# Opening of a fused LSH-attention and soft-MoE kernel: one load moves to ScalarE's queue, a cut at column 256, two spreads behind the shift's row, first maxima in the banks of two pools

## The chip, the cores and the metric

The kernel runs on one core of a Trainium2 chip. The metric is the device time of one execution in microseconds (us). A profiled execution has a span, from its first to its last instruction, and a time of its own, which is a little longer than the span. Engines are named as in the profile: PE (TensorE matmul), PEld (its weight loads), DVE (VectorE), ACT (ScalarE), POOL (GpSimd), SP (SyncE, which only issues DMAs here).

## The reference

There are 4 batches of 8 heads, 768 positions and 64 columns per head. For each head, positions are hashed to 6 bits, a query sees only keys of its own bucket, and the softmax output of the heads feeds a soft mixture of 8 experts with 4 slots each.

```python
q_bits = (np.einsum('bhsd,dk->bhsk', q, proj) > 0).astype(np.int64)
k_bits = (np.einsum('bhsd,dk->bhsk', k, proj) > 0).astype(np.int64)
...
mask = q_bucket[:, :, :, None] == k_bucket[:, :, None, :]
scores = scale * np.matmul(q, k.transpose(0, 1, 3, 2))
scores = np.where(mask, scores, -1000000000.0)
scores = scores - np.max(scores, axis=-1, keepdims=True)
attn = np.exp(scores)
attn = attn / (np.sum(attn, axis=-1, keepdims=True) + 1e-09)
return np.matmul(attn, v).astype(np.float32)
...
logits = x @ phi
...
slot_input = d.T @ x
...
h = np.maximum(slot_input[e] @ w1[e], 0.0)
slot_out[e] = h @ w2[e]
...
return (c @ slot_out).astype(np.float32)
```

## The kernel before

The 32 heads (4 batches times 8) are numbered h = 0 to 31 and are worked on one after the other, a pair (h, h+1) per load of q and k. Of each head, q and k are split into a high and a low part. They stand in two tiles, Y and X, which share one buffer `XY` per head; three such buffers (XY0, XY1, XY2) rotate, so heads 0 and 3 share XY0. Rows 64 to 79 of Y hold the hash bits in a form that pushes pairs of different buckets far down in the score.

For one head the steps are these. `smax` (line 463) makes a first, approximate score product on PE, 512 or 256 columns at a time, and DVE takes the largest value of each row (lines 477 and 480). `shift` (line 484) turns the maxima into one number per query on DVE (lines 489 to 492). `shift_rows` (line 496) transposes these numbers on PE (line 499), copies them with ACT into `mr` (line 502) and sends them by a DMA (`move`, line 379) into row 64 of the head's X and Y. This transfer is called the shift's row below, "XY<-mr" in the trace. Only then can `scores` (line 515 on PE, the exponential on ACT in line 519) start, since the row is part of its operands. `acc` (POOL) adds the row sums, `av` (line 544) multiplies with v.

Operands come to a head's buffer by DMAs that SP issues: `load` brings q and k of a pair (line 255), `spread_y`, `spread_l` and `spread_x` move parts of the stage into XY, `spread_bits` moves the bits from `bt` in four transfers, `load_v` brings v. SP takes them in the order in which they are issued in the program. An issue occupies SP's queue for some time, and an issue that waits holds all that stand behind it.

The order of the work is set by two tables, `STEADY` and `ONCE`, which give each call of a step a place in time; `at` looks a call up and the plan is sorted by that number. Entries far below zero belong to the opening, which is the time until head 0 has its maxima. Every engine gets its instructions in the order of the sorted plan.

In the opening the first pair is loaded in four halves (`load_half`, line 257): rows 0 to 63 (head 0) of k and of q, then rows 64 to 127 (head 1). `first_copy` (ACT, line 429) copies head 0's halves into Y. `first_bits` (line 435) projects them to bits on PE, 512 columns and then 256, and `first_over` (DVE, line 406) compares the result with the threshold and writes rows 64 to 79 of Y. `more_bits` (line 411) does the bits of both heads in one go. `first_hi` (ACT, line 440) and `split_lo` (POOL, line 375) make the high and low parts, and `first_x` (ACT, line 403) copies two of them into X. Between the steps, `spin` runs matmuls on a tile of ones that nobody reads, seven at the start and one or more after each maximum of head 0, so that PE has work.

The names in the trace: `st`, `smx`, `mi`, `av` are accumulation tiles in PSUM from the pools p_st (3 banks), p_sm (2), p_mi (2) and p_av (1); `mx` holds maxima, `stage` the raw and split q and k.

Of the kernel before, what the change touches and what calls it, by code (L numbers as in the profile page):

```python
# [9 lines left out]
F32 = mybir.dt.float32  # L10
F32R = mybir.dt.float32r
# [5 lines left out]
B, H, S, D, NB = 4, 8, 768, 64, 6  # L17
BH = B * H
P = 128
# [72 lines left out]
    ('first_copy', 1): -118.0, ('first_hi', 0): -107.0, ('first_hi', 1): -108.0, ('first_mz',): -96.0,  # L92
    ('first_over', 0, 0, 256): -110.0, ('first_over', 0, 256, 512): -100.0, ('first_over', 0, 512, 768): -99.0,
    ('first_over', 1, 0, 512): -111.0, ('first_over', 1, 512, 768): -109.0, ('first_rows', 0): -115.0,
    ('first_rows', 1): -114.0, ('first_rows', 2): -25.530842, ('first_x', 0): -83.0, ('first_x', 1): -78.0,
    ('keep_warm', 'c'): 195.7225, ('load', 10): 39.299177, ('load', 12): 51.299177, ('load', 14): 63.299177,
# [52 lines left out]
    ('spread_bits', 31): 174.191023, ('spread_bits', 4): 13.138864, ('spread_bits', 9): 42.191023,  # L149
    ('spread_l', 0): -91.0, ('spread_l', 1): -82.0, ('spread_l', 2): 1.51245, ('spread_l', 3): 6.331558,  # L150
    ('spread_x', 0): -87.0, ('spread_x', 1): -10.012043, ('spread_x', 2): 8.862333, ('spread_x', 3): 6.703225,
    ('spread_y', 1): -105.0, ('spread_y', 2): -86.0, ('spread_y', 25): 138.143568, ('spread_y', 27): 150.143568,
    ('spread_y', 29): 162.143568, ('spread_y', 3): 3.806412, ('spread_y', 31): 174.143568,
# [36 lines left out]
def lsh_attention_soft_moe(  # L190
# [11 lines left out]
    nc = tc.nc  # L202
# [43 lines left out]
    raw = stage[:, 0:2]  # L246
# [10 lines left out]
    def load_half(a):  # L257
        for x in (1, 0):
            nc.sync.dma_start(out=raw[D * a:D * a + D, x], in_=qk[x, 0, D * a:D * a + D])

# [4 lines left out]


    ones = cp.tile([P, 32], F32, name="ones")
    nc.vector.memset(ones, 1.0)
    XYs = [held.tile([P, 2, 2, S], F32R, name=f"XY{i}") for i, held in enumerate((yp, xp, yq))]
    Xs, Ys = [[t[:, :, n] for t in XYs] for n in range(2)]  # L270
    idle = Xs[2][:, 0, 0:P + 512]
    nc.vector.memset(idle.bitcast(F32), 1.0)
    eps = cp.tile([P, 1], F32, name="eps")
# [45 lines left out]

    def spin(n, cols=512):  # L320
        pt = p_av.tile([P, 512], F32, name="av")
        for _ in range(n):
            nc.tensor.matmul(pt[:, 0:cols], idle[:, 0:P], idle[:, P:P + cols], start=True, stop=True)

    spin(7)


# [93 lines left out]

    first_pt = {}

    def first_over(x, a, b):
        j = 2 * x + a // 512
        over(Ys[0][64:80, x, a:b], first_pt[x], slice(32 * j, 32 * j + 16), cols=slice(a % 512, a % 512 + b - a))

# [3 lines left out]
    def first_bits(x):  # L431
        first_pt[x] = p_st.tile([P, 512], F32, name="st")
        for c, (a, b) in enumerate(((0, 512), (512, S))):
            j = 2 * x + c
            nc.tensor.matmul(first_pt[x][32 * j:32 * j + 32, 0:b - a], pb[0:D, 32 * x:32 * x + 32], raw[0:D, x, a:b],
                             start=True, stop=True)
# [26 lines left out]
    def smax(h, t, part):  # L463
# [6 lines left out]
        if key not in s:  # L470
            s[key] = p_sm.tile([P, 512], F32, name="smx")
        pt = s[key]
# [8 lines left out]
        if h == 0 and t < NT - 1:  # L481
            spin(1)

# [381 lines left out]
    for n in (1, 0):  # L865
        at(first_copy, n)
        at(first_bits, n)
        at(first_hi, n)
    for xab in ((1, 0, 512), (0, 0, 256), (1, 512, S), (0, 256, 512), (0, 512, S)):
        at(first_over, *xab)  # L870
    at(more_bits)
    for n in range(3):
        at(spin, 2, tag=n)
    at(bits_rest)
# [264 lines left out]
```

## Time and profile before

| What | us |
|---|---|
| timed runs | 472.23, 474.15, 2233.8 |
| median of the three | 474.15 |
| profiled execution, its own time | 471.47 |
| its span | 469.7 |

Busy shares of the span are 97% for PE, 83% for DVE, 70% for POOL and 53% for ACT. The largest of the timed runs is far from all others, and the median of three is therefore one of two ordinary runs; the profiled execution is the lowest of the ordinary ones. The trace gives, for each instruction, its start from the beginning of the span, its duration, how long its engine was idle before it, and what ended that idle time.

### The profile page before, as it was taken

The page shows a single profiled execution, that of the slowest core. Times are in us where ns is not written, and L with a number is a line of the kernel's source. Part 1 is how long each engine was busy: PE and PEld are TensorE (multiplying, and loading weights), DVE is VectorE, ACT ScalarE, POOL GpSimd, SP SyncE. Part 2 cuts the span into 40 slices and gives each one's busy share as a digit, 9 for nine tenths or more (in the row PEclk, how much of TensorE's full clock was granted, in tenths as well). Part 3 has the DMA queues.
Part 4 walks back from the last instruction along what each step waited for, and adds up shares of the span by engine and source line. Part 5 has one row for each costly group of instructions (what it writes and reads, how often), then busy time and mean ns, then how long its engine had stood idle before and what let it go on. Part 6 is the DMA issues. An engine that isn't in the chain of part 4 may idle for free.

```text
span 469.7 us, 10655 instructions
## 1 busy us (share of the span) xinstructions
PE 456.4 (97%) x3980; PEld 287.8 (61%) x3980; DVE 389.0 (83%) x723; ACT 247.4 (53%) x462; POOL 327.6 (70%) x205
## 2 busy tenths in 40 slices
PE   7999999999999999999999999999999999999993
PEld 3565666666666666666656666666666666553472
DVE  7868898989798988889898989897979886787952
ACT  5364556464657555555556464646565545531242
POOL 7878778878775988787868987787759878810000
PEclk9999999999999999999999999999999999999998
DMA  5757677777774767878683878685846677899997
GB/s 159 200 139 165 162 170 230 163 238 164 218 172 150 170 194 165 238 167 241 145 235 106 205 203 202 206 202 159 200 135 166 177 180 258 297 387 409 408 365 305
DMA packets 39535, 99.29 MB, mean 211 GB/s; under 512 B 7326, under 2 KB 13612, under 8 KB 39484
## 3 DMA queue, kind: packets, MB, share of 16 engines
q1 hardware_dynamic: 39292, 98.16, 72.3%
q8 instruction: 31, 0.51, 0.4%
q10 hardware_dynamic: 160, 0.39, 0.4%
q14 instruction: 20, 0.16, 0.1%
q0 software_dynamic: 32, 0.07, 0.0%
HBM read 52.76 MB, written 6.29 MB: 126 GB/s over the span
## 4 chain that ended last, share of the span: by engine, by line
PE 91%; DVE 3%; DMA 2%; issue 1%; ACT 0%; SPq 0%; DVEq 0%; ACTq 0%
PE st L515 29%; PE av L544 25%; PE smx L474 16%; PE qs L1050 3%; PE qh L1000 3%; PE mi L556 2%; PE mi L411 2%; PE mi L607 2%; PE mi L572 2%; DMA XY<-mr 1%; PE mi L592 1%; DMA stage<-qk 1%; PE mi L762 1%; PE mi L499 1%; PE qh L1070 1%
## 5 line engine op out<-in xcount | busy, mean ns | idle before, releaser
L532 POOL TENSOR_TENSOR acc<-acc,pt 128x768 f32<-128x768 f32 x125 | 229.1, 1833 | 9.6
L519 ACT ACTIVATE pt<-st 128x512 f32<-128x512 f32 x288 | 164.3, 597 | 62.3 <-PE st L515 56.5
L515 PE MATMUL st<-XY 128*128 128x256 f32 (+1 forms) x768 | 178.0, 347 | 0.7 <-DMA XY<-mr 0.7
L480 DVE TENSOR_REDUCE mx<-smx 128x1 f32<-128x512 f32 x192 | 131.1, 688 | 24.9 <-PE smx L474 22.8
L515 PEld LDWEIGHTS st<-XY 128*128 128x128 f32 x768 | 125.0, 189 | 19.0 <-ACT pt L519 1.7
L544 PE MATMUL av<-pt,v 128*32 128x384 f32 x1536 | 133.1, 486 | 0.0
L474 PE MATMUL smx<-XY 96*128 96x512 f32 (+1 forms) x384 | 118.4, 357 | 1.2 <-DVE mx L477 0.9
L526 POOL TENSOR_TENSOR acc<-pt 128x768 f32<-128x768 f32 x32 | 58.9, 1839 | 53.1 <-ACT pt L519 53.1
L544 PEld LDWEIGHTS av<-pt,v 128*32 128x32 f32 x1536 | 49.7, 110 | 72.8 <-issue 71.6
L474 PEld LDWEIGHTS smx<-XY 96*128 96x128 f32 x384 | 66.0, 188 | 30.8 <-issue 9.6
L477 DVE TENSOR_REDUCE mx<-smx 128x2 f32<-128x512 f32 x96 | 65.8, 686 | 6.1 <-PE smx L474 5.5
L548 ACT COPY avs<-av 128x384 f32<-128x384 f32 x32 | 15.3, 477 | 82.9 <-PE av L544 82.8
L564 DVE RECIPROCAL dl<-sm 128x128 f32<-128x128 f32 x45 | 38.8, 915 | 13.9 <-ACT sm L559 10.1
L372 DVE TENSOR_REDUCE stage<-stage 128x768 fp32r<-128x1536 f32 x28 | 49.0, 1782 | 0.0
L365 ACT ACTIVATE stage<-stage 128x768 fp32r<-128x768 f32 x28 | 22.6, 836 | 5.3 <-DMA stage<-qk 3.8
L609 DVE TENSOR_TENSOR xq<-mi,r 128x256 f32<-128x256 f32 x45 | 17.4, 416 | 1.1 <-PE mi L607 1.1
L833 DVE STREAM_TRANSPOSE w<-call 32x256 f32<-32x256 f32 (+2 forms) x48 | 14.9, 333 | 1.7 <-PE qh L1000 1.1
L1050 PE MATMUL qs<-w 128*32 128x128 f32 (+1 forms) x352 | 15.3, 303 | 0.0
L607 PE MATMUL mi<-ident,avs 128*128 128x128 f32 x90 | 14.8, 272 | 0.0
L607 PEld LDWEIGHTS mi<-ident,avs 128*128 128x128 f32 x90 | 11.7, 140 | 4.0
L1050 PEld LDWEIGHTS qs<-w 128*32 128x32 f32 x352 | 10.6, 110 | 5.2 <-issue 2.2
L411 PE MATMUL mi<-stage,pb 128*32 128x384 f32 x120 | 12.8, 498 | 0.7 <-DMA stage<-qk 0.7
(183 smaller groups left out, 330.8 us busy)
## 6 DMA issues: line engine op xcount, KB each, us to landing
w<-w SPq DMA_DIRECT2D x53, 512.0 KB
XY<-stage SPq DMA_DIRECT2D x62, 384.0 KB
XY<-stage SPq DMA_DIRECT2D x62, 192.0 KB
stage<-qk SPq DMA_DIRECT2D x28, 384.0 KB
v<-vt SPq DMA_DIRECT2D x32, 192.0 KB
out<-stage SPq DMA_DIRECT2D x12, 512.0 KB
stage<-w SPq DMA_DIRECT2D x7, 512.0 KB
xq<-w SPq DMA_DIRECT2D x3, 512.0 KB
```

Source lines behind the costliest of these rows:

```text
L372: nc.vector.tensor_reduce(out=w[:, 2 * x + 1], in_=stage[:, x:n + 1:n - x].rearrange("p t s -> p s t"), axis=AX.X, op=ALU.add, negate=True)
L474: nc.tensor.matmul(pt[:, o:o + b - a], Ys[h % N_Y][0:96, 0, t * P:(t + 1) * P], Ys[h % N_Y][0:96, 1, a:b], start=True, stop=True)
L477: nc.vector.tensor_reduce(out=mx[:, n - 1:n + 1], in_=pt.rearrange("p (a x) -> p a x", a=2), axis=AX.X, op=ALU.max)
L480: nc.vector.reduce_max(out=mx[:, n:n + 1], in_=pt, axis=AX.X)
L515: nc.tensor.matmul(pt[:, o:o + b - a], x[:, 1, i * P:(i + 1) * P], x[:, 0, a:b], start=first, stop=not first)
L519: nc.scalar.activation(pts[i // 2][:, 512 * u:512 * u + 512], pt, AF.Exp, scale=D ** -0.5)
L526: nc.gpsimd.tensor_tensor(out=s["acc"], in0=pr[:, 0:S], in1=pr[:, S:2 * S], op=ALU.add)
L532: eng.tensor_tensor(out=s["acc"], in0=s["acc"], in1=pr[:, a * S:(a + 1) * S], op=ALU.add)
L544: nc.tensor.matmul(s["av"][D * c + d:D * c + d + 32, 0:HC], s["v"][:, i, d:d + 32], pr[:, o + c * HC:o + (c + 1) * HC], start=(i == 0), st ...
L564: nc.vector.reciprocal(out=st[h]["rs"][:, k * P:(k + 1) * P], in_=st[h]["sm"][:, k * P:(k + 1) * P])
L607: nc.tensor.transpose(pt[:, o:o + P], st[h + a]["avs"][:, k * P:(k + 1) * P], ident)
L1050: nc.tensor.matmul(po[32 * j:32 * j + 32], hTs[g][:, f, 32 * j:32 * j + 32], wt[1, x, 2 * g + f // 4, j].rearrange("p (f m) -> p f m", f=4 ...
```

## The change

Five things are edited, all in the first 20 us of the program:

1. The first half of k is loaded from ACT's DMA queue; the three other halves stay on SP's queue.
2. The bits of q are cut at column 256 and not at 512: PE projects 256 columns and then 512, and DVE's second comparison is one of 512 columns and not two of 256.
3. In the table, `spread_l` of head 1 and `spread_y` of head 2 come behind the shift's row of head 0 on SP's queue and not ahead of it, and the first of the two `first_x` copies comes ahead of ACT's two spreads.
4. The maxima of head 0 take their banks from p_sm and p_st in turn and not from p_sm alone.
5. The spins are 256 columns wide and twice as many; the tile of ones for them is filled first and is smaller.

```diff
-    ('spread_l', 0): -91.0, ('spread_l', 1): -82.0, ('spread_l', 2): 1.51245, ('spread_l', 3): 6.331558,
+    ('spread_l', 0): -91.0, ('spread_l', 1): -45.0, ('spread_l', 2): 1.51245, ('spread_l', 3): 6.331558,
...
     def load_half(a):
         for x in (1, 0):
-            nc.sync.dma_start(out=raw[D * a:D * a + D, x], in_=qk[x, 0, D * a:D * a + D])
+            eng = nc.scalar if x > a else nc.sync
+            eng.dma_start(out=raw[D * a:D * a + D, x], in_=qk[x, 0, D * a:D * a + D])
...
-    idle = Xs[2][:, 0, 0:P + 512]
+    idle = Xs[2][:, 0, 0:P + 256]
...
-    def spin(n, cols=512):
+    def spin(n, cols=256):
...
-    spin(7)
+    spin(14)
...
+    first_cuts = (0, 256, S), (0, 512, S)
 
     def first_over(x, a, b):
-        j = 2 * x + a // 512
-        over(Ys[0][64:80, x, a:b], first_pt[x], slice(32 * j, 32 * j + 16), cols=slice(a % 512, a % 512 + b - a))
+        c = first_cuts[x][1] <= a
+        j, o = 2 * x + c, a - first_cuts[x][c]
+        over(Ys[0][64:80, x, a:b], first_pt[x], slice(32 * j, 32 * j + 16), cols=slice(o, o + b - a))
...
-        for c, (a, b) in enumerate(((0, 512), (512, S))):
+        for c, (a, b) in enumerate(zip(first_cuts[x], first_cuts[x][1:])):
...
         if key not in s:
-            s[key] = p_sm.tile([P, 512], F32, name="smx")
+            pool = p_st if h == 0 and (key[1] + key[2]) % 2 else p_sm
+            s[key] = pool.tile([P, 512], F32, name=names[pool])
...
         if h == 0 and t < NT - 1:
-            spin(1)
+            spin(2)
...
-    for xab in ((1, 0, 512), (0, 0, 256), (1, 512, S), (0, 256, 512), (0, 512, S)):
+    for xab in ((1, 0, 512), (0, 0, 256), (1, 512, S), (0, 256, S)):
```

On SP's queue, around the shift's row of head 0. In the kernel before, XY_98, XY_99 and XY_100 are XY0, XY1 and XY2; the rows follow the load of `cst`:

```order
L379 DMA XY_99<-bt 13x384 x2
L379 DMA XY_99<-bt 12x384 x2
L379 DMA XY_100<-stage 64x2x768
L379 DMA XY_99<-stage 32x2x768
L379 DMA XY_98<-mr 1x12x128
L255 DMA stage<-qk 128x768 x2
```

In the changed kernel, where XY_96, XY_97 and XY_98 are XY0, XY1 and XY2:

```order
L380 DMA XY_97<-bt 13x384 x2
L380 DMA XY_97<-bt 12x384 x2
L380 DMA XY_96<-mr 1x12x128
L380 DMA XY_97<-stage 32x2x768
L380 DMA XY_98<-stage 64x2x768
L255 DMA stage<-qk 128x768 x2
```

The row of head 0 has moved ahead of the two spreads, which now stand between it and the load of the next pair; all that follows on SP is in the same order as before.

On DVE, from the first comparison of the bits to the fifth reduction of head 0. Before:

```order
L406 TENSOR_SCALAR XY_98<-st,con 16x512
L406 TENSOR_SCALAR XY_98<-st,con 16x256 x2
L480 TENSOR_REDUCE mx<-smx 128x1
L406 TENSOR_SCALAR XY_98<-st,con 16x256 x2
L477 TENSOR_REDUCE mx<-smx 128x2
L480 TENSOR_REDUCE mx<-smx 128x1 x2
L477 TENSOR_REDUCE mx<-smx 128x2
```

In the changed kernel:

```order
L407 TENSOR_SCALAR XY_96<-st,con 16x512
L407 TENSOR_SCALAR XY_96<-st,con 16x256 x2
L484 TENSOR_REDUCE mx<-smx 128x1
L407 TENSOR_SCALAR XY_96<-st,con 16x512
L481 TENSOR_REDUCE mx<-st 128x2
L484 TENSOR_REDUCE mx<-smx 128x1
L484 TENSOR_REDUCE mx<-st 128x1
L481 TENSOR_REDUCE mx<-smx 128x2
```

Two comparisons of 256 columns have become one of 512, and every second tile of maxima is an st tile.

## Rows read from the trace of the kernel before

**Rows 1.** Window: length; busy time by engine (instructions); granted clock; DMA share; GB/s.

```profile
44.00:419.00 375.00, 374.89 (x3136) 241.76 (x3137) 322.79 (x573) 210.98 (x395) 292.31 (x179) 1.00 0.71 194
```

**Rows 2.** Chain that ended last, 17 to 45: start, duration, what.

```profile
37.55 0.24 ACT mr L502
...
38.06 5.75 DMA XY<-mr
```

**Rows 3.** Timeline of PE: start, duration, operation, idle time before it.

```profile
43.85 0.73 PE L515 MATMUL st<-XY 128*128 128x512 f32 x2 [0.70 <-DMA XY<-mr]
```

**Rows 4.** Timeline of SP's queue, 0 to 46: start, duration of the issues.

```profile
1.18 2.49 SPq L259 DMA_DIRECT2D stage<-qk  x4
...
15.54 1.50 SPq L379 DMA_DIRECT2D XY<-stage  x2
18.04 0.82 SPq L379 DMA_DIRECT2D XY<-mr  x1
18.96 0.92 SPq L255 DMA_DIRECT2D stage<-qk  x2
19.97 3.26 SPq L379 DMA_DIRECT2D XY<-bt  x4
23.28 0.51 SPq L351 DMA_DIRECT2D v<-vt  x1
23.84 3.30 SPq L379 DMA_DIRECT2D XY<-stage  x3
27.24 0.83 SPq L379 DMA_DIRECT2D XY<-mr  x1
28.17 0.68 SPq L379 DMA_DIRECT2D XY<-stage  x1
28.89 4.36 SPq L379 DMA_DIRECT2D XY<-bt  x4
33.29 4.67 SPq L379 DMA_DIRECT2D XY<-stage  x5
38.06 1.80 SPq L379 DMA_DIRECT2D XY<-mr  x1
```

**Rows 5.** Waits of SP's queue, 0 to 45: total, times, longest.

```profile
SPq L379 <- ACT mr L502: 0.9, 1, 0.9
```

**Rows 6.** Chain that ended last, 0 to 44: its first steps.

```profile
3.08 4.29 DMA stage<-qk
7.41 0.85 PE mi L411 x8
```

**Rows 7.** Timeline of DVE, 6 to 21.

```profile
9.46 1.09 DVE L406 TENSOR_SCALAR XY<-st,con 16x256 fp32r<-16x256 f32 x2
...
12.76 0.69 DVE L477 TENSOR_REDUCE mx<-smx 128x2 f32<-128x512 f32 x1 [0.21 <-PE smx L474]
...
14.99 0.69 DVE L477 TENSOR_REDUCE mx<-smx 128x2 f32<-128x512 f32 x1 [0.25 <-PE smx L474]
15.90 0.69 DVE L480 TENSOR_REDUCE mx<-smx 128x1 f32<-128x512 f32 x1 [0.22 <-PE smx L474]
```

**Rows 8.** Groups of DVE by form, 6 to 18: busy us, mean ns, idle before.

```profile
L406 DVE TENSOR_SCALAR XY<-st,con 16x512 fp32r<-16x512 f32 x1 | 0.8, 807 | 1.3 <-ACT XY L429 1.3
```

**Rows 9.** Windows of two microseconds, columns as in rows 1.

```profile
4.00:6.00 2.00, 2.00 (x10) 0.63 (x9) 1.24 (x2) 1.43 (x2) 1.94 (x2) 1.00 1.01 230
...
23.00:25.00 2.00, 2.00 (x10) 1.50 (x9) 1.85 (x5) 1.79 (x4) 0.00 (x0) 1.00 0.26 68
...
35.00:37.00 2.00, 2.00 (x14) 1.77 (x13) 1.83 (x6) 1.89 (x4) 0.92 (x2) 1.00 0.94 203
```

**Rows 10.** Timeline of ACT, 0 to 22.

```profile
0.74 1.28 ACT L298 ACT_TABLE_LOAD   x1 [0.74 <-PEq L1130]
...
4.53 1.70 ACT L429 CAST XY<-stage 64x768 fp32r<-64x768 f32 x2 [1.74 <-DMA stage<-qk]
...
17.76 0.26 ACT L502 CAST mr<-mi 12x128 fp32r<-12x128 f32 x1 [1.43 <-PE mi L499]
```

More of the change, by code (lines that the diff above doesn't have):

```diff
@@ L92 @@
     ('first_copy', 1): -118.0, ('first_hi', 0): -107.0, ('first_hi', 1): -108.0, ('first_mz',): -96.0,
-    ('first_over', 0, 0, 256): -110.0, ('first_over', 0, 256, 512): -100.0, ('first_over', 0, 512, 768): -99.0,
+    ('first_over', 0, 0, 256): -110.0, ('first_over', 0, 256, 768): -100.0,
     ('first_over', 1, 0, 512): -111.0, ('first_over', 1, 512, 768): -109.0, ('first_rows', 0): -115.0,
-    ('first_rows', 1): -114.0, ('first_rows', 2): -25.530842, ('first_x', 0): -83.0, ('first_x', 1): -78.0,
+    ('first_rows', 1): -114.0, ('first_rows', 2): -25.530842, ('first_x', 0): -92.5, ('first_x', 1): -78.0,
     ('keep_warm', 'c'): 195.7225, ('load', 10): 39.299177, ('load', 12): 51.299177, ('load', 14): 63.299177,
@@ L149 @@
     ('spread_bits', 31): 174.191023, ('spread_bits', 4): 13.138864, ('spread_bits', 9): 42.191023,
-    ('spread_l', 0): -91.0, ('spread_l', 1): -82.0, ('spread_l', 2): 1.51245, ('spread_l', 3): 6.331558,
+    ('spread_l', 0): -91.0, ('spread_l', 1): -45.0, ('spread_l', 2): 1.51245, ('spread_l', 3): 6.331558,
     ('spread_x', 0): -87.0, ('spread_x', 1): -10.012043, ('spread_x', 2): 8.862333, ('spread_x', 3): 6.703225,
-    ('spread_y', 1): -105.0, ('spread_y', 2): -86.0, ('spread_y', 25): 138.143568, ('spread_y', 27): 150.143568,
+    ('spread_y', 1): -105.0, ('spread_y', 2): -44.9, ('spread_y', 25): 138.143568, ('spread_y', 27): 150.143568,
     ('spread_y', 29): 162.143568, ('spread_y', 3): 3.806412, ('spread_y', 31): 174.143568,
@@ L264, in lsh_attention_soft_moe @@
     vs = [held.tile([P, NT, D], F32, name=f"v{i}") for i, held in enumerate((ap, mp))]
+    XYs = [held.tile([P, 2, 2, S], F32R, name=f"XY{i}") for i, held in enumerate((yp, xp, yq))]
+    Xs, Ys = [[t[:, :, n] for t in XYs] for n in range(2)]
+    idle = Xs[2][:, 0, 0:P + 256]
+    nc.vector.memset(idle.bitcast(F32), 1.0)
     ones = cp.tile([P, 32], F32, name="ones")
     nc.vector.memset(ones, 1.0)
-    XYs = [held.tile([P, 2, 2, S], F32R, name=f"XY{i}") for i, held in enumerate((yp, xp, yq))]
-    Xs, Ys = [[t[:, :, n] for t in XYs] for n in range(2)]
-    idle = Xs[2][:, 0, 0:P + 512]
-    nc.vector.memset(idle.bitcast(F32), 1.0)
     eps = cp.tile([P, 1], F32, name="eps")
@@ L872, in lsh_attention_soft_moe @@
     for n in range(3):
-        at(spin, 2, tag=n)
+        at(spin, 4, tag=n)
     at(bits_rest)
```

## The prediction

> **What bounds the kernel now.** I began with the busy time by stretch. From 44 to 419 us PE is busy for 374.89 of 375.00 us [rows 1]: in four fifths of the span it waits for nothing, and the reader is to see that a gain of the opening reaches the end if, and only if, it reaches PE at 44 us. The change edits the first 20 us, so the question is what lies between.
>
> Next came the chain that ended last, between 17 and 45 us. It runs along PE, and then it has one large step that is not PE: 38.06 us, 5.75 us long, the shift's row of head 2 [rows 2]. On PE itself the same place shows as an idle time of 0.70 us in front of 43.85 us, ended by that transfer [rows 3]. So the scores of head 2 begin when a transfer lands, and PE would have been ready at 43.85 - 0.70 = 43.15 us.
>
> What sets that transfer? Its data were ready when ACT's copy ended, at 37.55 + 0.24 = 37.79 us [rows 2], and SP took it up at 38.06. The timeline of SP's queue tells why I don't read this as ACT's doing: from 18.96 to 38.06 us, which is 19.10 us, SP issues for 0.92 + 3.26 + 0.51 + 3.30 + 0.83 + 0.68 + 4.36 + 4.67 = 18.53 us [rows 4], and the issue before ended at 33.29 + 4.67 = 37.96 us. The queue is full from the load of the second pair on; what comes late at its beginning comes late at its end. In front of the row the DMA engines are full as well, with a share of 0.94 from 35 to 37 us [rows 9].
>
> The chain of the opening starts with the halves of q and k: the fourth lands at 3.08 + 4.29 = 7.37 us, and PE goes on with the bits at 7.41 us [rows 6].
>
> **The change part by part.** I count first what the row of head 0, issued at 18.04 us [rows 4], gains, and call that sum G.
>
> *The half of k on ACT's queue.* Four halves take 2.49 us of SP's queue, 0.62 us each [rows 4]; with one of them gone the last is issued 0.62 us earlier. That is the upper bound. The lower one comes from the DMA engines, which have a share of 1.01 from 4 to 6 us [rows 9]: if they are full from the first byte, all that helps is that the first byte is asked for at 0.74 us, where ACT's queue opens [rows 10], and not at 1.18 us [rows 4], 0.44 us. I take 0.55 us, between two ends that are close. On ACT the issue stands ahead of the table load, which would then start about 0.62 us later; ACT's copy of k waits 1.74 us for its data [rows 10], and that wait hides it.
>
> The Trainium skill, page "DMA: Bandwidth & Descriptors", section "Issuing engines are not separate DMA queues", says that DMAs started by different engines run on the same 16 DMA engines and that starting them from several engines saves only the time of starting them. By that rule alone this term would be 0.62 us, and the full share at 4 us speaks for less. With 0.62 the forecast below would fall by 0.07 us.
>
> *The cut at 256.* Two comparisons of 256 columns took 1.09 us [rows 7]; one of 512 columns takes 0.81 us [rows 8]. It stands between the first and the second maximum on DVE, which has work all along there: 0.28 us.
>
> *Two pools' banks.* What can go are DVE's waits for the next product, 0.21 + 0.25 + 0.22 = 0.68 us [rows 7]. The lower bound is 0, because the spins stand between the products as before and have as many columns (twice 256 for 512), so PE may set the same pace. I take the middle, 0.35 us: the bank was only one of two reasons.
>
> *The spins and ACT's copy.* The same columns, begun a little earlier: 0. The copy that goes ahead of ACT's spreads fills a stretch in which ACT waits; the row's copy on ACT waits 1.43 us for PE today [rows 10], so it costs nothing unless that wait is used up. 0.
>
> G = 0.55 + 0.28 + 0.35 = 1.18 us, with ends 0.44 + 0.28 + 0 = 0.72 and 0.62 + 0.28 + 0.68 = 1.58 us. The row of head 0 would be issued at 18.04 - 1.18 = 16.86 us.
>
> *The two spreads behind the row.* They took 1.50 us of SP's queue from 15.54 us on, and with the gap behind them 1.55 us [rows 4]. There they cost nothing, since SP then still waited 0.9 us for the row's data [rows 5]. Now SP waits idle and issues them after the row. Queued behind them is the load of the second pair, and behind that everything up to the row of head 2. The load, 0.92 us after the row today (18.96 - 18.04), now comes 0.92 + 1.55 us after it, at 16.86 + 2.47 = 19.33 us: 0.37 us **later** than before, though the row itself is 1.18 us earlier. The ends are 1.55 - 1.58 = -0.03 and 1.55 - 0.72 = +0.83 us.
>
> *From there to the end.* The full queue hands the 0.37 us on: the row of head 2 is issued at 38.43 and lands at 38.06 + 5.75 + 0.37 = 44.18 us. PE could start at 43.15 - 1.18 = 41.97 us at best and waits some 2.2 us instead of 0.70. All that head 0 won is given back there. Behind it PE is full as before, so the end moves by +0.37 us: 471.47 + 0.37 = 471.84 us for an execution like the profiled one (span 469.7, 1.8 us around it). The three ordinary runs shown are 471.47, 472.23 and 474.15 us; their middle one is 0.76 us above the profiled one, and the prediction is made for such a run: 472.23 + 0.37 = 472.6 us. By the ends of the sum alone it would lie between 472.2 and 473.1 us.
>
> **The rivals.**
>
> *The gain reaches the end.* If SP's queue has more slack than its issue times show (an issue of 1.80 us for a row of 12 pieces [rows 4] is time in which it was held up, not work), an earlier PE would bring the row of head 2 earlier, since its data were ready only 0.27 us before it was issued. Then the whole G stays: 472.23 - 1.18 = 471.05 us. For it speaks that the chain is PE and ACT up to 37.79 us [rows 2]; against it that the hold-ups come with a DMA share of 0.94 [rows 9], and the bytes in front of the row are as many as before and start later.
>
> *The transfers pile up, slower.* Place: the DMA engines behind the row of head 0. Until now they moved the two spreads while SP waited; now these start at about 16.86 + 0.92 = 17.8 us and not at 15.54, 2.24 us later, with the load right behind, and the bits of head 2 behind that. If nothing of this is made up, the row of head 2 lands 2.24 us later: 472.23 + 2.24 = 474.5 us. It decides once the pile is larger than the slack of the engines before 25 us; from 23 to 25 us their share is 0.26 [rows 9], which leaves 1.48 us. So most of it should be made up, and the price would be 0.76 us if the slack is used in full, hardly more than the forecast. For the full price the engines would have to be slow with small pieces there rather than idle.
>
> *The change doesn't do what it says.* The halves land no earlier, since two queues share the engines, and the spins keep PE's pace: G = 0.28 us, the load comes 1.55 - 0.28 = 1.27 us later, and the end is 472.23 + 1.27 = 473.5 us.
>
> **How the numbers follow.** I give the forecast 0.52, the gain that reaches the end 0.23, the pile 0.13, and no earlier landing 0.12. The likeliest case gives 472.6 us. The range must take in the first rival and the two slower ones with the scatter of single runs, 0.76 us below the middle one: 471.05 - 0.8 = 470.2 at the lower end, and 474.5 + 0.8 = 475.3 at the upper.
>
> About 2%, or 9.4 us, is what a measurement of this kernel can tell from no change. No case comes near it: all of the opening up to the row of head 0 is 18 us long and would have to be halved, or the stretch from 44 to 419 us, whose order of instructions the change leaves alone, would have to change. That gives 0.98 for within 2% and 0.01 for each side.
>
> **What would show it right or wrong.** In the profile of the changed kernel the row of head 0 should be issued between 16.5 and 17.3 us, the load of the second pair between 18.9 and 19.8 us, with SP idle for some 2 us ahead of the row. The row of head 2 should be issued at 38.0 us or later, and PE's idle time in front of its scores should have grown from 0.70 to about 2 us, now or spread over an earlier wait for the row of head 1. If the scores of head 2 start before 43.2 us, SP's queue was not the bound and the first rival holds. If PE waits at 25 us for the bits of head 2, or these scores start after 45 us, it is the pile. If the bits of both heads (the second line of rows 6) still start at 7.4 us, the halves did not land earlier. Any idle time of PE after 44 us that was not there before would make the step to the end wrong.

## The result: about 0.7% slower, and the profile after

| What | before | after |
|---|---|---|
| median of 12 runs, us | 471.82 | 475.95 |
| ratio, with its 95% interval | 1 | 1.0073 (1.0047 to 1.0098) |
| profiled execution, us | 471.47 | 474.60 |
| its span, us | 469.7 | 472.8 |

The forecast was 472.6 us, some 0.37 us above an ordinary run, with a range up to 475.3 us. The median of the changed kernel, 475.95 us, lies above that range; it is still within 2%. By the ratio the change costs 471.82 * 0.0073 = 3.4 us. The ratio leaves out the execution of 2233.8 us, and it is not the quotient of the two medians, which would be 1.0088.

The prediction's "load of the second pair" is the third load in the program, that of heads 4 and 5 (`load`, 4 in the table); q and k of heads 2 and 3 are loaded at 3.71 us. It is called the load of heads 4 and 5 below.

The timeline of SP's queue in the changed kernel, where the spreads now stand behind the row of head 0:

```profile
16.69 0.73 SPq L380 DMA_DIRECT2D XY<-mr  x1
17.52 1.49 SPq L380 DMA_DIRECT2D XY<-stage  x2
19.10 1.94 SPq L255 DMA_DIRECT2D stage<-qk  x2
21.14 3.92 SPq L380 DMA_DIRECT2D XY<-bt  x4
...
34.09 4.64 SPq L380 DMA_DIRECT2D XY<-stage  x5
39.79 0.92 SPq L380 DMA_DIRECT2D XY<-mr  x1
```

Against [rows 4] the row is 1.35 us earlier (18.04 to 16.69), the load starts only 0.14 us later (18.96 to 19.10), and then the queue loses time on issues that have not changed: the load takes 1.94 us and not 0.92, the four transfers of the bits of head 2 take 3.92 us and not 3.26. The last of these issues ends at 21.14 + 3.92 = 25.06 us; before, it ended at 19.97 + 3.26 = 23.23. That is 1.83 us later: 0.14 + 1.02 + 0.66, and 0.01 from rounding.

The windows of two microseconds show what the DMA engines did meanwhile, the kernel before first (the column next to the last is the share of the DMA engines):

```profile
15.00:17.00 2.00, 2.00 (x13) 0.83 (x13) 1.63 (x4) 1.33 (x2) 2.00 (x2) 1.00 0.62 141
17.00:19.00 2.00, 1.68 (x10) 0.91 (x6) 1.76 (x5) 0.26 (x1) 1.32 (x2) 1.00 0.97 181
19.00:21.00 2.00, 1.70 (x6) 0.86 (x7) 2.00 (x4) 0.00 (x0) 1.98 (x2) 1.00 0.67 200
21.00:23.00 2.00, 2.00 (x16) 1.87 (x16) 1.67 (x3) 1.28 (x3) 1.38 (x1) 1.00 0.81 317
```

and the changed kernel:

```profile
15.00:17.00 2.00, 1.43 (x11) 0.59 (x11) 1.03 (x5) 0.25 (x1) 2.00 (x2) 1.00 0.31 71
17.00:19.00 2.00, 1.75 (x9) 1.09 (x7) 2.00 (x4) 0.00 (x0) 1.72 (x3) 1.00 0.09 20
19.00:21.00 2.00, 1.81 (x14) 1.63 (x14) 1.98 (x4) 0.60 (x1) 1.94 (x2) 1.00 0.98 221
21.00:23.00 2.00, 2.00 (x12) 1.65 (x11) 1.96 (x4) 1.73 (x3) 0.49 (x1) 1.00 0.99 280
...
25.00:27.00 2.00, 0.00 (x0) 0.00 (x0) 0.00 (x0) 0.00 (x0) 1.92 (x2) 1.00 0.37 104
27.00:29.00 2.00, 1.79 (x13) 1.37 (x17) 1.29 (x2) 0.95 (x3) 1.92 (x2) 1.00 0.90 215
...
44.00:419.00 375.00, 373.22 (x3127) 239.95 (x3115) 321.33 (x568) 209.64 (x394) 292.19 (x177) 1.00 0.71 192
```

From 15 to 19 us the engines now do 2 * (0.62 + 0.97 - 0.31 - 0.09) = 2.38 us less of full work; the bytes of the two spreads come after 19 us, together with those of the load, and the share is 0.98 and 0.99 up to 23 us. The bits of head 2 come last in that pile. In windows of half a microsecond the full stretch ends at 22.5 us in the kernel before (first two lines) and at 24.0 us in the changed one (last two), 1.5 us later:

```profile
22.00:22.50 0.50, 0.50 (x6) 0.46 (x5) 0.47 (x2) 0.38 (x2) 0.41 (x1) 1.00 0.98 381
22.50:23.00 0.50, 0.50 (x4) 0.41 (x3) 0.50 (x1) 0.39 (x2) 0.00 (x0) 1.00 0.22 74
23.50:24.00 0.50, 0.50 (x4) 0.30 (x3) 0.43 (x3) 0.50 (x2) 0.00 (x0) 1.00 0.97 366
24.00:24.50 0.50, 0.31 (x3) 0.11 (x1) 0.06 (x1) 0.50 (x2) 0.00 (x0) 1.00 0.11 28
```

The chain that ended last, from 0 to 28 us, now runs through them:

```profile
2.44 4.41 DMA stage<-qk
...
22.95 1.34 SPq L380
...
24.34 2.67 DMA XY<-bt
27.01 0.20 issue
27.21 0.47 PE smx L478
```

On the timeline of PE the first maximum of head 2 waits for them:

```profile
27.21 0.47 PE L478 MATMUL smx<-XY 96*128 96x512 f32 x1 [2.89 <-DMA XY<-bt]
```

In the kernel before, the same product followed its predecessor with no idle time:

```profile
25.31 0.40 PE L474 MATMUL smx<-XY 96*128 96x512 f32 x1
```

So PE came to it 25.31 - (27.21 - 2.89) = 0.99 us earlier than before, and left it 1.90 us later. The 0.70 us in front of the scores of head 2 [rows 3] are gone, and these scores start 1.10 us later than before, without a wait:

```profile
44.95 0.63 PE L519 MATMUL st<-XY 128*128 128x512 f32 x2
```

The rest of the loss comes after 44 us. There PE is busy for 373.22 us where it was for 374.89 [rows 1], and the waits of PE from 44 to 419 us in the changed kernel are these (total, times, longest), none of which stood there before:

```profile
PE smx L478 <- DMA XY<-bt: 1.1, 1, 1.1
PE smx L478 <- DVE mi L493: 0.5, 1, 0.5
PE smx L478 <- DVE mx L481: 0.2, 1, 0.2
```

1.10 us at the scores of head 2 and 374.89 - 373.22 = 1.67 us of PE's busy time make up 2.8 of the 3.1 us between the two spans.

### The profile page after: what moved, and what is told of

Read it like the earlier page. It is cut to its first block, busy times and chain, and to the rows that moved or that the text cites. A ratio compares the mean times of both kernels' runs of the same rounds, so it can differ in the third digit from the quotient of the medians.

```text
span 472.8 us, 10698 instructions
## 1 busy us (share of the span) xinstructions
PE 456.0 (96%) x4003; PEld 290.3 (61%) x4003; DVE 388.3 (82%) x722; ACT 246.9 (52%) x462; POOL 327.3 (69%) x205
## 4 chain that ended last, share of the span: by engine, by line
PE 87%; DVE 4%; DMA 3%; SPq 2%; issue 1%; POOL 1%; ACT 0%; DVEq 0%; POOLq 0%
PE st L519 27%; PE av L548 25%; PE smx L478 15%; PE qs L1054 3%; PE qh L1004 3%; PE mi L560 2%; PE mi L412 2%; PE mi L611 2%; PE mi L576 2%; SPq L380 2%; DMA XY<-bt 2%; PE mi L596 1%; DMA stage<-qk 1%; PE mi L766 1%; PE mi L503 1%
## 5 line engine op out<-in xcount | busy, mean ns | idle before, releaser
L484 DVE TENSOR_REDUCE mx<-smx 128x1 f32<-128x512 f32 x190 | 129.6, 688 | 29.8 <-PE smx L478 27.1
L478 PE MATMUL smx<-XY 96*128 96x256 f32 (+1 forms) x378 | 116.2, 357 | 5.4 <-DMA XY<-bt 4.3
L478 PEld LDWEIGHTS smx<-XY 96*128 96x128 f32 x378 | 64.9, 188 | 34.3 <-issue 9.9
L481 DVE TENSOR_REDUCE mx<-smx 128x2 f32<-128x512 f32 x94 | 64.3, 685 | 4.4 <-PE smx L478 3.8
```

The source lines that it names most:

```text
L478: nc.tensor.matmul(pt[:, o:o + b - a], Ys[h % N_Y][0:96, 0, t * P:(t + 1) * P], Ys[h % N_Y][0:96, 1, a:b], start=True, stop=True)
L481: nc.vector.tensor_reduce(out=mx[:, n - 1:n + 1], in_=pt.rearrange("p (a x) -> p a x", a=2), axis=AX.X, op=ALU.max)
L484: nc.vector.reduce_max(out=mx[:, n:n + 1], in_=pt, axis=AX.X)
```

## Experiments

Each ratio is to the kernel before, run beside it on the same chip. Four of the runs are a second look at a kernel that had run already. The "mean clock" of an execution is PE's granted clock averaged over all of it, as a share of full speed.

**The spreads back ahead of the row**, all else as in the changed kernel:

```diff
-    ('spread_l', 1): -45.0
+    ('spread_l', 1): -82.0
...
-    ('spread_y', 2): -44.9
+    ('spread_y', 2): -86.0
```

> The changed kernel with one part undone: the two spreads stand ahead of head 0's shift row on SP's queue again, as in the kernel before; the other four edits stay. Theory P (pile: behind the row the spreads start late, the load and the bits of head 2 queue behind them, PE waits for the bits): the 2.89 us wait of PE for the bits of head 2 at 24.3 us is gone, the spreads are issued within SP's wait for the row, from about 15.1 us, the load of the second pair comes at about 17.7 us (18.96 before, 19.10 in the changed kernel), the scores of head 2 start at 42.6 to 43.2 us, and the time is 1 to 1.2 us below the kernel before, ratio to it 0.997 to 0.999. Rival Q (the load on ACT's queue, the new cut or the two pools' banks cost the time): the wait or another one stays and the ratio is 1.005 or more. Rival C (the time is lost to the granted clock and not to the transfers): the runs' clocks stay below 0.995 and the ratio above 1.003.

Measured: 474.61 us, 1.0063 (1.0042 to 1.0083), six executions. The wait for the bits of head 2 is gone from the profile, and still most of the slowdown was there. That made the spreads look innocent, wrongly in part, as later runs show. The condition of rival C was met as well: five of the six executions have a mean clock of 0.984 to 0.993, and in the profile the granted clock is 0.61 in the mean from 20 to 24 us.

**The spreads alone**, moved in the kernel before:

```diff
-    ('spread_l', 1): -82.0
+    ('spread_l', 1): -45.0
...
-    ('spread_y', 2): -86.0
+    ('spread_y', 2): -44.9
```

> The kernel before with that one part alone: spread_l of head 1 and spread_y of head 2 behind the shift's row of head 0, everything else as before. Theory P: with the row issued at about 18 us the spreads start at about 18.9 us and the load at about 20.5 us, the bits of head 2 land 1 to 1.5 us later than the 27.0 us of the changed kernel, PE waits 2 to 3.5 us for them at about 25.3 us, and the time is 2.5 to 5 us above the kernel before (ratio 1.005 to 1.011), at least as slow as the changed kernel. Rival Q: no more than 0.5 us from the kernel before, ratio 0.999 to 1.001.

Measured: 474.43 us, 1.0058 (1.0035 to 1.0080), six executions. The timeline of PE shows the wait:

```profile
27.03 0.47 PE L474 MATMUL smx<-XY 96*128 96x512 f32 x1 [2.04 <-DMA XY<-bt]
```

The move alone makes the wait, and in these six executions it costs nearly as much as all of the change.

**The load of heads 4 and 5 behind the bits of head 2**, in the changed kernel:

```diff
-    ('load', 4): -24.143741
+    ('load', 4): -23.0
```

> The changed kernel with the load of the second pair moved behind the four transfers of the bits of head 2 on SP's queue; the spreads stay behind the row. It tells what of the pile the bits wait for: the two spreads or the load. If the load (786 KB in front of the bits on the same queue) is what they wait for, the bits are issued from 19.1 to 22.3 us and land by 24.3 us, PE's wait falls from 2.89 us to under 0.3 us, and the scores of head 2 start at 43.2 to 44.2 us, by the row of head 2 as in the kernel before: ratio 0.999 to 1.002. If the spreads alone fill the engines, PE still waits 1 us or more for the bits: ratio 1.004 to 1.008.

Measured: 474.63 us, 1.0070 (1.0042 to 1.0097). Waits of PE, 20 to 45 us:

```profile
PE st L519 <- DMA XY<-bt: 3.2, 1, 3.2
PE smx L478 <- DMA XY<-bt: 0.6, 1, 0.6
```

The first wait shrinks to 0.6 us, and one of 3.2 us stands in front of scores in its place: the pile is only reordered. The first wait can't be compared by its length alone, since PE was slower at the head in this execution: the row of head 0 was issued at 19.02 us, and PE came to the product at 26.16 and not at 24.32 us. From the issue of the row to the waiting product it is 7.77 us here and 9.16 to 10.52 us in the five profiles with the spreads and this load in front of the bits, so the load has its share in the pile.

**The two spreads behind the row, issued from ACT's queue:**

```diff
-        move(Ys[h % N_Y][0:64], st[h]["w4"][r:r + 64, 0::2])
+        move(Ys[h % N_Y][0:64], st[h]["w4"][r:r + 64, 0::2], nc.scalar if h == 2 else nc.sync)
...
-        move(Ys[h % N_Y][96:128], s["w4"][r:r + 32, 1:3], nc.sync if h else nc.scalar)
+        move(Ys[h % N_Y][96:128], s["w4"][r:r + 32, 1:3], nc.sync if h > 1 else nc.scalar)
```

> The changed kernel with the two spreads at their new place behind the row, but issued from ACT's queue, where ACT waits for the first scores anyway. It tells whether SP's issue order or the DMA engines make the bits late. If SP's queue does: the load is issued at about 17.5 us, the bits of head 2 from 18.5 us, they land by 24 us, no wait of PE over 0.3 us, and the scores of head 2 start at 42.7 to 43.5 us: ratio 0.997 to 1.000. If the DMA engines do (the bytes start late whichever queue they come from): the bits still land behind spreads and load, about 1.5 us earlier than 27.0 us, PE waits 1 to 1.5 us: ratio 1.001 to 1.004.

Measured: 473.26 us, 1.0036 (1.0009 to 1.0063). PE still waits at the same place:

```profile
26.97 0.47 PE L478 MATMUL smx<-XY 96*128 96x512 f32 x1 [1.35 <-DMA XY<-bt]
```

SP's queue no longer carries the spreads, and 1.35 us of wait stay. That the wait is shorter than 2.89 us is mostly PE's doing: the granted clock was 0.57 from 8 to 12 us in this execution, and PE came to the product at 25.62 us and not at 24.32. The product starts only 0.24 us earlier (26.97 against 27.21). Spreads and load are issued at about the same times as there (17.89 and 19.00 against 17.52 and 19.10 us) and the last of the bits 1.20 us earlier, by 23.86 us, and still they land hardly earlier. The share of the DMA engines is 0.94 up to 24.0 us and 0.22 in the next half microsecond, the same end as there. So the work put off on the engines makes the wait, more than the order on SP's queue. The Trainium skill, page "DMA: Bandwidth & Descriptors", section "Issuing engines are not separate DMA queues", says that transfers of different issuers run on the same engines. The trace agrees: with another issuer the landing moves by 0.24 us.

**The half of k on ACT's queue alone**, in the kernel before:

```diff
-            nc.sync.dma_start(out=raw[D * a:D * a + D, x], in_=qk[x, 0, D * a:D * a + D])
+            eng = nc.scalar if x > a else nc.sync
+            eng.dma_start(out=raw[D * a:D * a + D, x], in_=qk[x, 0, D * a:D * a + D])
```

> The kernel before with one edit alone: the first half of k is loaded from ACT's queue. After the four runs above, with the spreads in their old place still 3 us slow, the theory is K: an edit of the opening leaves PE with less dense work in some stretch of its first 40 us, the granted clock then falls to 0.5 for 3.4 us in more of the runs, and PE loses about half of such a stretch each time. By K this edit lengthens PE's wait for the bits (0.66 us in the kernel before) or leaves it, and the runs' mean clock falls from 0.996 to below 0.994 if it is the cause, with a ratio of 1.003 or more. Rival W (small waits between 44 and 419 us, which the profile of the kernel before does not have, cost the time): PE's idle time there exceeds 0.5 us. Rival N (harmless): ratio 0.998 to 1.001, clock 0.995 or more.

Measured: 470.88 us, 0.9996 (0.9979 to 1.0013). It does no harm, and its 0.5 us does not show at the end.

**The two pools' banks alone:**

```diff
-            s[key] = p_sm.tile([P, 512], F32, name="smx")
+            pool = p_st if h == 0 and (key[1] + key[2]) % 2 else p_sm
+            s[key] = pool.tile([P, 512], F32, name=names[pool])
```

> The kernel before with one edit alone: the maxima of head 0 take banks of p_sm and p_st in turn. PE's wait of 0.72 us at 10.6 us for a bank should go. Theory K: PE is then done with head 0 earlier and thinner later; if this edit is the cause, mean clock of the runs below 0.994 and a ratio of 1.003 or more. Rival W: idle time of PE over 0.5 us between 44 and 419 us. Rival N: ratio 0.998 to 1.001.

Measured: 472.19 us, 1.0020 (0.9999 to 1.0041). No gain either. (The mean clock of the twelve is 0.992, that of the kernel before beside them 0.996.)

**The narrow spins alone**, in the kernel before:

```diff
-    idle = Xs[2][:, 0, 0:P + 512]
+    idle = Xs[2][:, 0, 0:P + 256]
-    def spin(n, cols=512):
+    def spin(n, cols=256):
...
```

with 14, 2 and 4 spins where there were 7, 1 and 2.

> The kernel before with one edit alone: spins of 256 columns, twice as many (and the smaller tile of ones). The columns are the same, so by the sum of the prediction nothing changes. Theory K: if two short spins count for less than one long one, the clock falls more often; mean clock of the runs below 0.994, ratio 1.003 or more. Rival W: idle time of PE over 0.5 us between 44 and 419 us. Rival N: ratio 0.998 to 1.001.

Measured: 474.41 us, 1.0072 (1.0045 to 1.0098), six executions from 472.32 to 475.63 us, with a mean clock of 0.990. By this run the spins looked like the whole cause.

**The kernel before, once more, as if it were a changed one:**

> The kernel before, unchanged, as a kernel of its own: a second trace of it and a control of the comparison. Ratio 0.999 to 1.001. Theory K: no stretch of granted clock 0.5 between 8 and 460 us in its trace, or one that costs under 1.7 us. Rival W is tested here: if its trace too has PE idle for 0.5 to 2 us between 44 and 419 us, such waits are chance of a run and no effect of the change; if PE is idle for under 0.3 us there as in the first trace, they belong to the changed opening.

Measured: 471.56 us, 1.0008 (0.9989 to 1.0026): no difference between the places of a kernel in the comparison. Its profile, too, has no wait of PE from 46 to 418 us (busy 371.80 of 372.00 us), so the waits there are not found in either profile of the kernel before. Its head is another matter, as told further below: the row of head 0 is issued at 19.69 us, 1.65 us later than in the first profile.

**The spins put back in the changed kernel**, 512 columns wide and half as many, the spreads left behind the row:

```diff
-    def spin(n, cols=256):
+    def spin(n, cols=512):
-    spin(14)
+    spin(7)
...
```

> The changed kernel with the spins' width and number put back (512 columns, 7 at the start, 2 a call, 1 between the first maxima), and nothing else. Theory N (the narrow spins are the main cause: the spins alone cost 1.0072): what is left is the two spreads behind the row with the earlier row, so TensorE still waits 2 to 3 us for the bits of head 2, and the ratio falls from 1.0073 to between 1.000 and 1.005. Rival P (the pile of transfers is the main cause, the spins' cost being of another kind that does not add): 1.006 to 1.009, unchanged. If the ratio lies below 0.998, both were wrong: then the spins alone ate a real gain.

Measured: 473.66 us, 1.0053 (1.0028 to 1.0079), with a wait of 1.99 us for the bits of head 2. This is just above what was expected with the narrow spins as the main cause (up to 1.005), and just short of the rival's 1.006. Most of the loss is here without them.

**Both put back**, so that the earlier load, the cut, the banks and the earlier copy on ACT are left:

```diff
-    ('spread_l', 1): -45.0
+    ('spread_l', 1): -82.0
...
-    ('spread_y', 2): -44.9
+    ('spread_y', 2): -86.0
...
-    def spin(n, cols=256):
+    def spin(n, cols=512):
...
```

> The changed kernel with the spins put back and the two spreads put back ahead of the row: what is left is the load of k's halves on the two queues, the cut at column 256, and the two pools' banks. Theory N: neither costly part is in it, so 0.997 to 1.000 (the earlier row is worth at most 1 us at the head, 0.998, if none is given back). Rival W (whatever starts the steady stretch about 1 us earlier meets VectorE or a transfer later and gives it back, and lowers the clock on the way): 1.003 to 1.006, as with the spins narrow and the spreads back (1.0063).

Measured: 471.45 us, 0.9999 (0.9980 to 1.0018). The loss is gone. The waits of PE from 46 to 418 us are gone with it; its busy time there is 371.82 of 372.00 us (371.89 in the kernel before):

```profile
46.00:418.00 372.00, 371.82 (x3114) 238.82 (x3114) 320.89 (x569) 208.87 (x394) 290.67 (x177) 1.00 0.71 194
```

**Narrow spins by parts**, in the kernel before. First everywhere but at the start:

```diff
-            spin(1)
+            spin(2, 256)
...
-        at(spin, 2, tag=n)
+        at(spin, 4, 256, tag=n)
```

> The kernel before with narrow spins (256 columns, twice as many) everywhere but in the first call, which keeps 7 of 512. The spins alone cost 1.0072 with all of them narrow. If the place where they hurt is between the bits and the first maxima (7 to 15 us), where each is one more instruction between two that VectorE waits for: 1.005 to 1.008 here and 0.999 to 1.001 with only the first call narrow. If the first call is the place (where the granted clock first rises): 0.999 to 1.002 here.

Measured: 471.84 us, 1.0025 (1.0006 to 1.0044). Then only at the start:

```diff
-    spin(7)
+    spin(14, 256)
```

> The kernel before with only the first call of spins narrow (14 of 256 columns in place of 7 of 512; the tile that they read is as wide as before, so they start no earlier). If the first call is the place where narrow spins hurt: 1.005 to 1.008; if it is the spins behind the bits and between the first maxima: 0.999 to 1.001. If both this and the run with the others narrow stay under 1.002, it is neither alone: then the smaller tile and the earlier start, which neither of the two has, are what is left.

Measured: 471.75 us, 1.0014 (0.9999 to 1.0029). Neither half gives the 1.0072.

**Matmuls in the wait.** In the kernel with wide spins, nine products of 512 columns that nobody reads stand ahead of the waiting maximum; in the changed kernel itself, eighteen of 256:

```diff
+    def spin_wait(n, cols=512):
+        pt = p_av.tile([P, 512], F32, name="av")
+        for _ in range(n):
+            nc.tensor.matmul(pt[:, 0:cols], Ys[0][:, 1, 0:P], Ys[0][:, 0, 0:cols], start=True, stop=True)
...
+        if h == 2:
+            plan.append((1.5114, len(plan), (spin_wait, 9)))
```

> The changed kernel with wide spins (1.0053 in its own run, with TensorE's wait of 1.99 us for the bits of head 2 and a granted clock of 0.5 for 3.41 us from 27.44 us), and 9 more matmuls of 512 columns, on rows of head 0, just ahead of the waiting first maximum: some 1.9 us of TensorE work that nothing needs, in the wait. Theory K (a part of the cost is the clock that falls behind the wait): the wait is as long, but the clock no longer falls at 27 us in the profile, and the ratio comes down to 1.001 to 1.003. Rival W (the wait itself, and TensorE's further waits, are the whole cost): 1.0045 to 1.006, or more if the added matmuls run past the landing.

> The changed kernel itself with 18 more matmuls of 256 columns in TensorE's wait for the bits of head 2 (2.89 us there in its profile). Theory K: the part of its 1.0073 that is the clock behind the wait goes, 1.003 to 1.006. Rival W: 1.0065 to 1.008, unchanged. If the narrow spins cost by themselves in the same runs, and not by the same wait, what is left here is near their ratio alone.

Measured: 473.92 us, 1.0054 (1.0029 to 1.0079, eight executions) and 473.11 us, 1.0039 (1.0021 to 1.0058). The first profile, taken of the shortest of its eight executions, on the timeline of PE:

```profile
24.01 2.21 PE L329 MATMUL av<-XY 128*128 128x512 f32 x9
...
26.98 0.47 PE L483 MATMUL smx<-XY 96*128 96x512 f32 x1 [0.76 <-DMA XY<-bt]
```

and the window behind it, with the granted clock in the third column from the end:

```profile
27.00:29.00 2.00, 2.00 (x13) 1.38 (x17) 1.50 (x3) 1.18 (x3) 1.92 (x2) 1.00 0.87 220
```

The same window of the kernel without these products:

```profile
27.00:29.00 2.00, 1.71 (x7) 1.64 (x8) 0.69 (x1) 0.61 (x2) 1.92 (x2) 0.61 0.79 204
```

In the filled wait the clock stays at 1.00 in this execution, where it fell to 0.61 of full speed in the mean of that window without the filling. The ratio is 1.0054 against 1.0053. But this does not test the clock as a cause: over all executions the mean clock is 0.993 with the filling and 0.992 without it, and 0.992 both ways in the other pair (1.0039 against 1.0073 and, below, 1.0062, where the intervals overlap). What is shown is that the filling bought no time. Another reading of the record bounds the clock's part. Of the twelve executions with wide spins and the spreads behind the row, the four with a mean clock of 0.994 or more took 474.14 us on average and the other eight 473.90, so the cost of the spreads is there without a fall of the clock. In the changed kernel the executions with 0.994 or more took 474.29 us (five) in the first run and 472.89 (four) in the second, below, and the others of each ratio 476.50 and 475.18. Beside the second run the kernel before took 471.04 us at such clocks. With narrow spins a part of the loss may thus be the clock's. How large it is stays open.

**Narrow spins on a tile as wide as before**, so that they start no earlier (both edits by parts, together):

```diff
-    spin(7)
+    spin(14, 256)
...
-            spin(1)
+            spin(2, 256)
...
-        at(spin, 2, tag=n)
+        at(spin, 4, 256, tag=n)
```

> The kernel before with all spins narrow, but reading from a tile as wide as before, filled in the same place, so that they start no earlier (the two runs with a part of the spins narrow gave 1.0025 and 1.0014, the one with the narrow tile 1.0072). If the width itself costs and the parts add up: 1.003 to 1.005. If the earlier start by 0.27 us is what costs: 1.000 to 1.002. If they do more together than alone: 1.006 to 1.008.

Measured: 472.52 us, 1.0024 (1.0006 to 1.0041). Beside it **the narrow spins alone, again**:

> The spins of the change alone, once more, beside the run with the tile left wide: its six executions lay from 472.32 to 475.63 us, and its profile was taken of the shortest. If its 1.0072 holds: 1.005 to 1.009, and the profile shows either a stretch at a granted clock of 0.5 in the first 45 us, or TensorE's waits for VectorE and transfers near 132 and 371 us, or both. If the six executions were the long ones by chance: 1.001 to 1.004.

Measured: 471.82 us, 1.0009 (0.9991 to 1.0026), twelve executions. The 1.0072 of the first run, on another chip, does not hold; the two intervals don't even touch. What was built on it (that the spins are the main cause) falls.

**The first experiment again, and the changed kernel again beside it:**

> The changed kernel with the two spreads back ahead of the row, once more, with more executions and beside the changed kernel: its first run gave 1.0063 in six executions, but the narrow spins, which that run had left as the suspect, gave 1.0009 when they were run again, and the same kernel with wide spins gave 0.9999. Theory S (the spreads behind the row are the cause, and the six executions were long by chance): 0.998 to 1.003 here. Theory N (the narrow spins cost only together with the earlier load and the banks): 1.005 to 1.008, as before.

> The changed kernel itself, beside the one with the spreads back, on the same chip. Theory S: 1.004 to 1.008, at least 0.003 over the other. Theory N: both alike within 0.002, at 1.005 to 1.008. If both lie under 1.003, the slowdown of the first comparison was in part chance too.

Measured: spreads back 472.47 us, 1.0034 (1.0011 to 1.0057); changed kernel 474.26 us, 1.0062 (1.0037 to 1.0087), twelve executions each. The slowdown repeats. With the spreads back about half of it goes. The 1.0034 lies between what the two theories allowed (up to 1.003 and from 1.005): the spreads are a cause, and something is left when only they are put back. What is left stands after 46 us; the profile of that run has PE busy for 370.32 us there, with these waits:

```profile
PE smx L478 <- DVE mz L496: 0.7, 1, 0.7
PE smx L478 <- DVE mz L494: 0.5, 1, 0.5
PE smx L478 <- DVE mi L493: 0.5, 1, 0.5
```

The new profile of the changed kernel has the wait for the bits again, 2.71 us, and this time the clock falls behind it:

```profile
25.00:27.00 2.00, 0.29 (x1) 0.32 (x2) 0.00 (x0) 0.00 (x0) 1.92 (x2) 0.82 0.42 119
27.00:29.00 2.00, 2.00 (x8) 1.81 (x8) 1.11 (x2) 0.73 (x2) 1.92 (x2) 0.50 0.95 206
29.00:31.00 2.00, 2.00 (x10) 0.50 (x13) 0.97 (x2) 1.45 (x3) 1.92 (x2) 0.50 0.72 184
...
33.00:35.00 2.00, 2.00 (x32) 0.76 (x24) 0.00 (x0) 0.00 (x0) 0.98 (x1) 0.97 0.14 38
```

Its span is 474.8 us, 2.0 us more than that of the first profile, in which the clock stayed up.

**Together.** With the earlier load, the cut and the banks in all of them:

| | spreads ahead of the row | spreads behind it |
|---|---|---|
| wide spins | 0.9999 | 1.0053 |
| narrow spins | 1.0063 and 1.0034 | 1.0073 and 1.0062 |

Shown is that the spreads behind the row cost some 0.5%, 2.5 us, where the spins are wide: 0.9999 (0.9980 to 1.0018) and 1.0053 (1.0028 to 1.0079), twelve executions each, side by side. The spreads alone on the kernel before agree with it, 1.0058, in six executions that were not repeated. With narrow spins the difference is 0.1% and 0.3%, and the intervals overlap. Every profile with the spreads there, eight of eight with the runs that change something around them, has PE waiting for the bits of head 2 or the wait filled by added products, and no profile with the spreads ahead has one. The narrow spins add between 0.1% and 0.6% by company and run, and the two don't add up. What the spins do is not settled: the profiles with narrow spins and the spreads ahead differ from the kernel before in waits of PE for DVE of 0.2 to 0.8 us near 133, 161 and 372 us, and these differ from one profile to the next.

## Why the prediction was wrong, point by point

*The head.* The row of head 0 was forecast for 16.86 us and was issued at 16.69. The halves landed at 2.44 + 4.41 = 6.85 us against 7.37 [rows 6], 0.52 us for a term of 0.55. The rule on issuing engines from the Trainium skill, page "DMA: Bandwidth & Descriptors", section "Issuing engines are not separate DMA queues", would have given 0.62 us. The cut, from the timeline of DVE, and the waits that are left between maxima of the two pools:

```profile
8.92 0.81 DVE L407 TENSOR_SCALAR XY<-st,con 16x512 fp32r<-16x512 f32 x1
...
13.63 0.69 DVE L481 TENSOR_REDUCE mx<-st 128x2 f32<-128x512 f32 x1 [0.19 <-PE st L478]
14.55 0.69 DVE L484 TENSOR_REDUCE mx<-smx 128x1 f32<-128x512 f32 x1 [0.23 <-PE smx L478]
```

0.81 for 1.09 us is the 0.28 forecast. Of the waits [rows 7], 0.21 + 0.25 + 0.22 us, there remain 0.19 + 0.23, so the banks gave 0.26 us for a term of 0.35. The sum G came to 18.04 - 16.69 = 1.35 us where 1.18 was forecast, within its ends. In these two profiles the head did what was asked, and the error lies behind it. That the 1.35 comes so near the forecast is luck in part, since the head of one kernel varies by more than that. The eight products of the bits took 0.85 us in both, but 1.51 us in the second profile of the kernel before, where the row came at 19.69 us, and 1.51 us with both edits put back, where it came at 19.55: between these two the edits that are left bring it forward by 0.14 us. The second profile of the changed kernel has the faster products and the row at 16.82.

*The step that failed: "There they cost nothing, since SP then still waited 0.9 us", and what follows from it, "The full queue hands the 0.37 us on".* The spreads had used engines that were otherwise idle between 15 and 19 us; I priced only their place in SP's queue. The load of heads 4 and 5 was forecast for 19.33 us and came at 19.10, so the sum over SP's queue was right to 0.23 us up to there. But it kept the issue times behind the load as they were, and the load's 0.92 became 1.94 and the bits' 3.26 became 3.92 us, 1.68 us that the sum did not have. The load's part goes with the spreads: 0.92 to 0.95 us in all twelve profiles with the spreads ahead of the row, 1.91 to 1.97 in the six with the spreads right in front of it on SP's queue, and 1.05 with the spreads on ACT's queue, at a DMA share of 0.94. So it is not the share alone that holds SP up. Nor is it only SP: in that run the last of the bits were issued 1.20 us earlier and landed 0.24 us earlier, behind the same work on the engines. The bits' part can't be put on the spreads: it is 3.26 to 4.09 us with the spreads ahead and 3.33 to 4.09 with them behind. Nor did the full queue act up to the row of head 2: that row was issued at 39.79 us, later than the 38.43 forecast, and SP's queue stood idle from 34.09 + 4.64 = 38.73 us until then. The delay came through PE, which had waited at 24.32 us.

*The place.* I followed the queue to the row of head 2 at 38 us, where PE waited before, and passed over the first user on the way, the first maximum of head 2 at 25.31 us. It showed no wait, which tells only that the slack was not negative. There the whole pile met PE: 2.89 us.

*The rival that named it.* "The transfers pile up, slower" had the place, PE waiting at 25 us for the bits of head 2, and its full price, 474.5 us, is near the 474.60 of the profiled execution. That nearness is luck: the price was a row of head 2 that lands 2.24 us later, on a base of 472.23 us, and the scores of head 2 start 1.10 us later, with the rest lost after 44 us. The rival got 0.13 because I let 1.48 us of empty engine time between 23 and 25 us [rows 9] make most of it up. That time lies behind the bits and can't help them. Its condition should have been read in the windows from 19 to 23 us, with shares of 0.67 and 0.81, that is 2 * (0.33 + 0.19) = 1.04 us of room for 2.38 us of work put off. The 1.34 us that this leaves compare with the 1.5 us by which the full stretch ended later.

*From there to the end.* "Behind it PE is full as before" failed too: 1.67 us less of PE's busy time between 44 and 419 us. The prediction named this as what would make the step wrong. Why PE meets DVE and transfers there, in kernels whose order behind 44 us is the same, is not shown; the runs say only that it is absent from the profile in which both edits are undone.

*The spins, costed at 0* ("The same columns, begun a little earlier"). Alone they are 0 within the interval (0.9991 to 1.0026) in the longer run. With the earlier load and banks, and the spreads ahead, narrow spins gave 1.0034 and 1.0063 where wide ones gave 0.9999, so the 0 was too low there by 1.6 to 3.0 us, through a mechanism that I can't name; of the two intervals that of 1.0034 still touches the one of 0.9999.

*The first rival,* that the gain reaches the end, is refuted for the change as it was made. In its pure form it was not tested: with both costs put back the ratio is 0.9999, but the profile of that kernel has no gain at the head to hand on (the row at 19.55 us against 18.04 and 19.69 in the two profiles of the kernel before).

## What to carry to other kernels

Price a transfer that is moved later by the engine time it leaves idle, and compare that with the room between its new place and the first thing that needs a transfer queued behind it; room further on does not count. An issue time in a profile is not a constant to add up: the same load took 0.92 us of SP's queue or 1.94, by what stood in front of it. A wait that shrinks must be read with the time at which the waiting engine came, not by its length alone. And for effects of half a per cent, a comparison of six executions can mislead by its whole size: repeat it before building on it.

## What the runs showed of the hardware that was not expected

- PE's granted clock fell to 0.50, the lower of its two levels (1.2 GHz), behind a wait of 2 to 3 us that had followed dense work, and came back a few microseconds later; in the second profile of the changed kernel it is 0.50 from 27 to 33 us. It need not happen: the first profile has a wait of 2.89 us and stays at 1.00 behind it, in the windows from 25 to 29 us and from 44 to 419.
- PE's pace in the first 13 us differs between executions, at a granted clock of 1.00 in the rows of both: the eight products of the bits take 0.85 us in the first profile of the kernel before and 1.51 us in the second. Why is not shown.
- Between an issue and its bytes lies more than the issue: the spreads issued from 17.52 to 19.01 us leave the DMA share at 0.09 from 17 to 19 us, and it is 0.98 in the next two.
- The same kernel, the narrow spins alone, gave 1.0072 (1.0045 to 1.0098) in six executions and 1.0009 (0.9991 to 1.0026) in twelve. The scatter between groups of executions is larger than the intervals within one say.
